# Forgetting attention and a SwiGLU block on one core: the seven-product output projection begins one token tile earlier, and three due times move

## The chip, the cores and the metric

The kernel runs on one core of a Trainium2 chip. The core has TensorE (PE, matrix products into PSUM), VectorE (DVE) and ScalarE (ACT), which read and write PSUM and SBUF, GpSimd (POOL), which here works on SBUF alone, and SyncE (SP), which issues DMAs. Each engine works through its own list of instructions in order. Semaphores make an instruction wait for another engine or for a DMA. The metric is the device time of one execution in microseconds, as the median of several runs.

## The reference

Inputs are q, k and v of 8 batches x 8 heads x 576 positions x 64, a forget gate f per position, and three weight matrices, w_gate and w_val (512 x 1536) and w_out (1536 x 512).

```python
scores = (1 / 8) * q @ k.T
cum    = cumsum(log(clip(f, 1e-4, 1)), axis=-1)
scores = where(causal, scores + cum[:, None] - cum[None, :], -1e9)
attn   = softmax(scores) @ v                          # per batch and head
x      = attn.transpose(0, 2, 1, 3).reshape(4608, 512)
g      = x @ w_gate
out    = (g * sigmoid(g) * (x @ w_val)) @ w_out       # 4608 x 512, float32
```

## The kernel before

The attention works on heads; a pair of heads shares one transposed tile of q and k (`QK`), with four more rows for the decay. Head h belongs to batch h // 8, pair p to batch p // 4. The scores of one head are computed with keys on the partitions, in four groups, called score banks here, each of which fills part of one PSUM bank (L703, `score`). ACT takes the exponent into `PT` or, for the first group, `PTa` (L737). POOL zeroes what lies above the diagonal (L746, `mask`). PE weighs the values with it (L760, `weigh`); a column of ones beside the values gives the denominator. DVE takes the reciprocal (L767) and scales (L772, into `xn`). The result is turned by a DMA transpose (L790, `cross`) or by PE (L777, `flip`, and a copy, `put`) into `xT`, the input of the second half. Two PSUM banks hold scores, one holds the weighed values, four serve the second half ("f"), one serves turning.

The loads of a pair p from 8 on have three steps: POOL issues DMAs that write q and k to DRAM as bf16 (L590, `narrow`); SP issues two DMA transposes from there into `QK` (L599, `turned`) and then a DMA for the decay rows (L602, `rows`).

The second half goes over nine tiles of 512 tokens, tiles 0 to 8. For each of 12 column blocks of 128 there are four matmuls with w_gate (`gp`) and four with w_val (`vp`), all L918; ACT takes the tanh (L922; Silu from tile 6 on, L925); DVE forms g * sigmoid(g) (L932, `silu`; not where ACT takes Silu) and multiplies (L935, `mul`) into `HH`. Two column blocks share one `HH` buffer.

The output projection of a tile comes in two forms. The plain form (`simple`, L976) has, for each of its two halves q and each of two token groups, 12 matmuls of 512 columns; ACT copies the result out of PSUM (L979), and SP stores it. The other form (`finish`, L969) computes a 2 x 2 block product with seven products in place of eight. For it, DVE adds parts of the activations (L960, `sums`: per `HH` buffer two of 512 columns and one of 256, into `SU`), and the weights are added once per run (L948 and L950, `blend`: six into `wt`, and four that overwrite quarters of `wo` and so come behind the last plain projection). Each product is six matmuls of 256 columns. ACT (L982), POOL (L989 `both`, L1014 `apart`) and DVE (L993 `more`, L1017 `close`) put the seven products together, and SP stores (L1020).

The order of all of this is made when the program is built, by the class `Plan`: a list of operations with engines, estimated durations, dependencies, buffers to take, a key and a time from which an operation may start (`ready`). It plays the list through and lets each engine take the ready operation with the lowest key; the order found is the order of the instructions in each engine's list. On the chip only the order is left: an operation starts when those before it on its engine are done and its semaphores allow it. Two of the times are of use below. `release(p)` is when the transposes of pair p become due, `release(p) - LEAD` when its narrowing DMAs do:

```python
release = lambda p: 0.0 if p < 2 * FB else PACE0 + min(p - 2 * FB, FB) * PACE_A + max(p - 3 * FB, 0) * PACE
for r in tails[:QUICK]:
    simple(*r)
blended = [op(..., blend, n, after=ready, key=BLEND_KEY + n, ready=BLEND_AT, ...) for n in range(6)]
blended += [op(..., blend, n, after=blended[:6] + plain, ...) for n in range(6, 10)]
for r in tails[QUICK:]:
    finish(*r, blended)
```

FB is 4, the pairs of a batch. With the constants before, pair 8 is due at 59.0, pair 12 at 95.0, and each later pair 8.6 after the one before it. Keys of activation sums (50000) and of weight sums (40000) are high, so DVE takes them when nothing else is ready.

Of the kernel before, what the change touches and what calls it, by code (L numbers as in the profile page):

```python
# [212 lines left out]
CROSS = (8, 9, 10)  # L213
PACE = 8.6
LATE = 2.5
PACE_A = 9.0
PACE0 = 59.0
LEAD = 14.0


@with_exitstack
def kernel(ctx, tc, q, k, v, f, w_gate, w_val, w_out, out):
# [81 lines left out]
    def op(eng, fn, *args, tag=None, packet=20.0, **kw):  # L304
        if not isinstance(eng, dict):
            eng = {eng[0]: eng[1]}
        o = plan.op(eng, lambda e: fn(e, *args), **kw)
        o.tag, o.packet = tag, packet
        return o
# [237 lines left out]
    for h, name, i in fixed + [(hqk[FB + p], "qk", 2 + p) for p in range(FB)]:  # L547
        h.pool, h.i = name, i
        plan.free[name].remove(i)
    release = lambda p: 0.0 if p < 2 * FB else PACE0 + min(p - 2 * FB, FB) * PACE_A + max(p - 3 * FB, 0) * PACE  # L550

# [127 lines left out]
    def queries(p, key):  # L679
        narrowed = [op(("POOL", SW), narrow, p, x, key=key - 200 + x, ready=release(p) - LEAD, dma=1.1, packet=900, tag=("narrow", p))  # L680
                    for x in range(2)]
        ts = []
        for x in range(2):
            ts.append(op(("SP", 1.45), turned, p, x, after=[narrowed[x], o_edge] + out1, behind=ts, take=[] if x else [hqk[p]],
                         use=[hqk[p]] if x else [], key=key, dma=1.6, ready=release(p), tag=("turned", p)))
        done = ts + [op(("SP", SPi), rows, p, after=ts + out0 + out1 + o_out2, use=[hqk[p]], key=key + 3, dma=0.25,
                        tag=("rows", p))]
        for j in range(2):
            q_ready[2 * p + j] = done
# [369 lines left out]
    def ffn(t, t0, n):  # L1059
        key, hs, ms = 1e5 * (t + 1), [None] * (KF // 2), []  # L1060
        for fc in range(KF):
            parts = [(0, HALF), (HALF, n - HALF)] if t == 0 and fc < WIDE else [(0, n)]
            ms.append([])
            for u, (lo, w) in enumerate(parts):
                lg, m = unit(t, fc, t0 + lo, w, hs, lo, key + 100 * fc + 50 * u, [last_gate[0]])
                ms[fc].append(m)
        last_gate[0] = lg
        tails.append((t, t0, key, hs, ms))
# [3 lines left out]
    def simple(t, t0, key, hs, ms):  # L1072
        for q in range(2):
            bo = Buf("ot")
            for h in range(2):
                bf, a = Buf("f"), None
                for g in range(0, KF // 2, 2):
                    a = op(("PE", mm(*[DM] * 4)), project, hs, q, h, bf, (g, g + 1),
                           after=[x for m in ms[2 * g : 2 * g + 4] for x in m] + [w_ready["o", c] for c in range(NCO)] + [a],
                           take=[] if g else [bf], use=[hs[g], hs[g + 1]] + ([bf] if g else []), key=key + 2000 + 200 * q + 100 * h + g, tag=("fo", t, q, h))  # L1080
                plain.append(a)
                c = op(("ACT", act(DM)), out_copy, h, bf, bo, after=[a] + (o_out2 + regrouped if t == 0 else []), take=[] if h else [bo],
                       use=[bf] + ([bo] if h else []), key=-4, tag=("ot", t, q, h))
                op(("SP", 0.7), store, t0 + h * HALF + q * P, h, bo, after=[c], use=[bo], key=-4, dma=1.0, packet=90, tag=("out", t, q, h))
# [92 lines left out]
    for t, t0 in enumerate(range(0, N_TOK, MT)):  # L1177
        ffn(t, t0, MT)
    for r in tails[:QUICK]:
        simple(*r)  # L1180
    ready = [w_ready["o", c] for c in range(NCO)]
    blended = [op({e: f((KF // 2) * HALF // 2) + 0.35 * (n // 2 == 1) for e, f in BLEND_ON.items()}, blend, n, after=ready, key=BLEND_KEY + n, ready=BLEND_AT, tag=("blend", n)) for n in range(6)]
    blended += [op({e: f((KF // 2) * HALF // 2) for e, f in BLEND_ON.items()}, blend, n, after=blended[:6] + plain, key=BLEND_KEY + n, ready=BLEND_AT, tag=("blend", n)) for n in range(6, 10)]
    for r in tails[QUICK:]:
        finish(*r, blended)
# [16 lines left out]

QUICK = 3


def F_POOLS(t):
# [19 lines left out]
BOTH_ON = {"POOL": pool2}  # L1228
APART_ON = {"POOL": pool2}
BLEND_ON = {"DVE": fast}  # L1230
BLEND_AT = 150.0
POOL_KEY = 50000
ALONE = (6, 6)
LAST_ON = {"DVE": slow}
# [126 lines left out]
```

## Time and profile before

| what | value |
|---|---|
| median of 3 runs (lowest to highest) | 378.81 us (378.62 to 379.19) |
| the profiled execution | 378.57 us |
| its span | 376.9 us |
| PE busy | 368.7 us, 98% |
| DVE busy | 248.9 us, 66% |
| ACT busy | 214.3 us, 57% |
| POOL busy | 161.4 us, 43% |
| granted TensorE clock | 1.00 in every stage |

The profile shows one execution. A row of a group gives line, engine, operation, tiles, shapes and count, then busy time in us and the mean duration of one in ns, then the idle time of the engine just before, and what ended it. A row of a time line gives start and duration in us. A shown matmul is longer than its share of TensorE's time, since the next one starts while it drains; from start to start is what counts. Busy shares are averages over stages with different limits. The stage up to about 288 us holds attention and tiles 0 to 6 side by side; what comes after is tiles 6 to 8 alone.

### The profile page before, as it was taken

Reading aid. Unit: us, or ns where it says so; the run is one execution under the profiler, and the core shown is the slowest. Engines: PE = TensorE matmul, PEld = TensorE weight load, DVE = VectorE, ACT = ScalarE, POOL = GpSimd, SP = SyncE. Lnnn points to the kernel's source line nnn. Section 1 sums busy time; section 2 is a strip of 40 time slices with the busy share of each in tenths; the row PEclk is TensorE's granted clock in tenths of the full one; section 3 lists DMA queues with packets and bytes.
Section 4 is the critical chain, followed back from the end, with each engine's and each line's share of the span. In section 5 each row is a group of like instructions: output and inputs, shape, how many; then the busy total and the mean of one; then the engine's idle time right before and its main releaser. Section 6 shows DMA issues by size and latency. Waiting matters only on the chain.

```text
span 376.9 us, 9094 instructions
## 1 busy us (share of the span) xinstructions
PE 368.7 (98%) x3427; PEld 233.7 (62%) x3427; DVE 248.9 (66%) x575; ACT 214.3 (57%) x438; POOL 161.4 (43%) x388
## 2 busy tenths in 40 slices
PE   8899999999999999999999999999999999999995
PEld 5667665455565555555685458655887776467464
DVE  7878986177526674499737994598638844753664
ACT  7999952265756754746576467555774433323322
POOL 8897547033633643465376437742462012003000
PEclk9999999999999999999999999999999999999999
DMA  8999998969988998998599999994225003002003
GB/s 147 192 197 195 207 200 151 167 117 176 177 186 169 199 164 151 227 189 183 117 155 206 220 132 165 241 222 95 60 73 93 2 2 111 2 0 89 25 0 114
DMA packets 125178, 52.01 MB, mean 138 GB/s; under 512 B 111838, under 2 KB 119710, under 8 KB 124366
## 3 DMA queue, kind: packets, MB, share of 16 engines
q1 hardware_dynamic: 108638, 36.08, 48.5%
q0 software_dynamic: 16288, 15.14, 27.2%
q8 instruction: 27, 0.44, 0.5%
q10 hardware_dynamic: 208, 0.20, 0.2%
q14 instruction: 17, 0.14, 0.1%
HBM read 38.56 MB, written 17.07 MB: 148 GB/s over the span
## 4 chain that ended last, share of the span: by engine, by line
PE 94%; DVE 2%; ACT 2%; issue 1%; POOL 0%; DVEq 0%
PE ps L918 49%; PE ps L969 14%; PE ps L703 10%; PE ps L976 8%; PE ps L760 8%; PE ps L721 1%; PE ps L777 1%; PE ps L578 1%; PE ps L729 0%; ACT QK L327 0%; ACT PT L737 0%; ACT PTa L737 0%; DVE hh L935 0%; ACT L530 0%; PE ps L1195 0%
## 5 line engine op out<-in xcount | busy, mean ns | idle before, releaser
L918 PE MATMUL ps<-xT,wv 128*128 128x512 bf16 (+2 forms) x496 | 111.8, 352 | 0.0
L918 PE MATMUL ps<-xT,wg 128*128 128x512 bf16 (+2 forms) x496 | 111.6, 352 | 0.0
L737 ACT ACTIVATE PT<-ps 128x384 bf16<-128x384 f32 (+2 forms) x192 | 91.7, 510 | 14.8 <-PE ps L703 9.7
L935 DVE SCALAR_TENSOR_TENSOR hh<-th,ps 128x512 bf16<-128x512 f32 (+1 forms) x112 | 74.5, 667 | 21.1 <-PE ps L918 12.9
L922 ACT ACTIVATE th<-ps 128x512 f32<-128x512 f32 (+1 forms) x82 | 47.2, 577 | 54.2 <-PE ps L918 51.8
L746 POOL TENSOR_SCALAR_AFFINE_SELECT PT<-PT 128x128 bf16<-128x128 bf16 (+1 forms) x192 | 54.1, 288 | 44.1 <-ACT PT L737 38.5
L918 PEld LDWEIGHTS <-wv 128*128 128x128 bf16 x496 | 45.0, 97 | 38.1
L918 PEld LDWEIGHTS <-wg 128*128 128x128 bf16 x496 | 45.1, 97 | 37.9
L932 DVE SCALAR_TENSOR_TENSOR th<-th,ps 128x512 f32<-128x512 f32 (+1 forms) x82 | 53.7, 656 | 19.7 <-ACT th L922 19.5
L703 PE MATMUL ps<-QK 68*128 68x256 bf16 x392 | 64.0, 261 | 0.4 <-ACT PTa L737 0.4
L746 POOL TENSOR_SCALAR_AFFINE_SELECT PTa<-PTa 128x256 bf16<-128x256 bf16 x64 | 26.3, 414 | 81.2 <-ACT PTa L737 80.4
L760 PE MATMUL ps<-VB,PT 128*128 128x65 bf16 x768 | 42.1, 193 | 0.0
L703 PEld LDWEIGHTS <-QK 68*128 68x128 bf16 x392 | 31.5, 97 | 14.0 <-issue 0.6
L760 PEld LDWEIGHTS <-PT 128*128 128x128 bf16 x768 | 34.2, 97 | 9.3 <-POOL PT L746 0.9
L737 ACT ACTIVATE PTa<-ps 128x384 bf16<-128x384 f32 x64 | 30.9, 487 | 15.6 <-PE ps L703 14.8
L767 DVE RECIPROCAL rc<-ps 128x5 f32<-128x5 f32 (+2 forms) x68 | 12.8, 188 | 40.4 <-PE ps L760 40.0
L969 PEld LDWEIGHTS <-su 128*128 128x128 bf16 x360 | 34.8, 97 | 4.6
L960 DVE TENSOR_TENSOR su<-hh 128x512 bf16<-128x512 bf16 (+1 forms) x108 | 36.7, 384 | 0.9
L925 ACT ACTIVATE th<-ps 128x512 f32<-128x512 f32 x30 | 17.9, 596 | 32.1 <-PE ps L918 32.1
L976 PE MATMUL ps<-wo,hh 128*128 128x512 bf16 x144 | 34.8, 379 | 0.0
L772 DVE TENSOR_TENSOR xn<-ps,rc 128x320 bf16<-128x320 f32 (+2 forms) x72 | 32.4, 454 | 2.2
L969 PE MATMUL ps<-wt,su 128*128 128x256 bf16 x216 | 28.8, 272 | 0.0
(97 smaller groups left out, 322.1 us busy)
## 6 DMA issues: line engine op xcount, KB each, us to landing
out_dram<-ot SPq DMA_DIRECT2D x34, 256.0 KB
natv<-in_v_dram SPq DMA_DIRECT2D x25, 256.0 KB
qk_d<-in_q_dram POOLq DMA_DIRECT2D x24, 144.0 KB, 3.6
qk_d<-in_k_dram POOLq DMA_DIRECT2D x24, 144.0 KB, 4.4
wv<-in_moe_w_val_dram POOLq DMA_DIRECT2D x3, 512.0 KB, 10.4
wg<-in_moe_w_gate_dram POOLq DMA_DIRECT2D x3, 512.0 KB, 12.2
wo<-in_moe_w_out_dram POOLq DMA_DIRECT2D x4, 384.0 KB, 13.8
VB<-in_v_dram POOLq DMA_DIRECT2D x7, 128.0 KB, 9.1
```

The lines of the kernel that those rows point to most:

```text
L703: nc.tensor.matmul(s[:, c : c + w], QK[:KR, hqk[p].i, 1, j * S + kt * P : j * S + (kt + 1) * P], QK[:KR, hqk[p].i, 0, j * S + q0 : j * S + ...
L737: nc.scalar.activation(place(h, i)[:, OFFS[i] : OFFS[i] + c], ps(bs)[:, :c], AF.Exp, scale=0.125)
L746: nc.gpsimd.affine_select(out=d, in_=d, pattern=pat, compare_op=ALU.is_ge, fill=0.0, base=0, channel_multiplier=-1,)
L760: nc.tensor.matmul(o[:, lo : lo + D + 1], pt[:, c : c + P], VB[hvb[b].i][:, kt, hb, : D + 1], start=first and n == 0, stop=last and n == l ...
L772: nc.vector.tensor_mul(XN[bx.i][:, qb : qb + nq, j], o, r)
L918: nc.tensor.matmul(ps(bf)[:, a:b], w[:, ko, fc * P : (fc + 1) * P], xT[:, ko, at : at + b - a], start=ko == 0 and a == 0, stop=ko == KD - ...
L922: nc.scalar.activation(TH[bt.i][:, :n], ps(bf)[:, :n], AF.Tanh, scale=0.5)
L932: nc.vector.scalar_tensor_tensor(out=t, in0=t, scalar=1.0, in1=ps(bf)[:, :n], op0=ALU.add, op1=ALU.mult)
L935: nc.vector.scalar_tensor_tensor(out=HH[bh.i][:, r, lo : lo + n], in0=TH[bt.i][:, :n], scalar=by, in1=ps(bf)[:, :n], op0=ALU.mult, op1=ALU ...
L960: E[e].tensor_tensor(out=o, in0=x, in1=y, op=f)
L969: nc.tensor.matmul(ps(bf)[:, c * HALF : (c + 1) * HALF], left(g)[:, q * P : (q + 1) * P], right[:, g], start=opens and g == 0, stop=g == K ...
L976: nc.tensor.matmul(ps(bf), HH[hs[g].i][:, r, lo : lo + P], wo[:, 2 * g + r], start=g + r == 0, stop=2 * g + r == KF - 1)
```

## The change

Six constants change; no function does. `QUICK`, the number of tiles with the plain projection, goes from 3 to 2, so tile 2 is projected with seven products. `BLEND_AT`, from which the weight sums may start, goes from 150 to 100. `PACE0` and `PACE_A` make pair 8 due at 57.0 instead of 59.0, with 8.8 instead of 9.0 from there to pair 12 (92.2 instead of 95.0), and 8.6 behind that as before. `LEAD` lets the narrowing DMAs be due 13.0 ahead of their pair instead of 14.0. Since the planner plays the whole list through anew, the order of instructions on all engines differs from where tile 1's projection and the third batch meet.

```diff
@@ -213,9 +213,9 @@
 CROSS = (8, 9, 10)
 PACE = 8.6
 LATE = 2.5
-PACE_A = 9.0
-PACE0 = 59.0
-LEAD = 14.0
+PACE_A = 8.8
+PACE0 = 57.0
+LEAD = 13.0
@@ -1202,7 +1202,7 @@
-QUICK = 3
+QUICK = 2
@@ -1228,7 +1228,7 @@
 BLEND_ON = {"DVE": fast}
-BLEND_AT = 150.0
+BLEND_AT = 100.0
 POOL_KEY = 50000
```

## The prediction

> **What bounds the kernel now.** I read the page first (busy shares, then the chain that ended last), then the table of stages, then the time lines of the few places where TensorE stood still.
>
> ```profile
> span 376.9 us, 9094 instructions
> PE 368.7 (98%) x3427; PEld 233.7 (62%) x3427; DVE 248.9 (66%) x575; ACT 214.3 (57%) x438; POOL 161.4 (43%) x388
> ...
> PE 94%; DVE 2%; ACT 2%; issue 1%; POOL 0%; DVEq 0%
> ```
>
> TensorE (PE) is the bound: 98% of the span, and 94% of the chain that ended last. The profiled execution took 378.57 us, 1.7 us more than its span; the median of the runs shown is 378.81, 0.24 above it. So the time after is this one's 378.57, less TensorE work removed, plus TensorE holes added, less holes that go; 0.24 on top gives the median. About 0.2% (0.76 us) is what a measurement of this kernel can tell from no change.
>
> The stages from 160 us on, columns window, width, busy time of PE, weight loads, DVE, ACT and POOL, then granted clock, DMA share, GB/s:
>
> ```profile
> 160.00:180.00 20.00, 19.44 (x147) 10.29 (x146) 19.06 (x39) 10.80 (x24) 11.52 (x25) 1.00 1.07 185
> 180.00:200.00 20.00, 19.48 (x219) 15.34 (x217) 10.66 (x28) 14.01 (x30) 12.30 (x30) 1.00 0.85 150
> 200.00:240.00 40.00, 39.88 (x366) 25.54 (x364) 29.06 (x63) 24.09 (x50) 21.95 (x54) 1.00 1.09 180
> 240.00:300.00 60.00, 60.00 (x609) 41.70 (x606) 45.30 (x100) 37.17 (x76) 22.86 (x59) 1.00 0.52 107
> ```
>
> VectorE (DVE) is full at 160 to 180 us, which is the stage of tile 3: ten weight sums, that tile's activation sums and the attention beside them. There and just behind it TensorE loses its time. On TensorE's time line the three places are these:
>
> ```profile
> 176.78 1.03 PE L918 MATMUL ps<-xT,wv 128*128 128x512 bf16 x4
> 178.37 0.25 PE L760 MATMUL ps<-VB,PTa 128*128 128x65 bf16 x3 [0.56 <-DVE xn L772]
> ...
> 182.27 0.55 PE L703 MATMUL ps<-QK 68*128 68x256 bf16 x4
> 183.18 0.33 PE L703 MATMUL ps<-QK 68*128 68x64 bf16 x2 [0.36 <-ACT PTa L737]
> 183.66 0.27 PE L760 MATMUL ps<-VB,PTa 128*128 128x65 bf16 x3 [0.15 <-POOL PTa L746]
> ...
> 208.89 1.03 PE L918 MATMUL ps<-xT,wv 128*128 128x512 bf16 x4
> 210.04 0.25 PE L760 MATMUL ps<-VB,PTa 128*128 128x65 bf16 x3
> ```
>
> Starts tell more than busy time here, since a matmul's shown end overlaps the next. Four matmuls of 512 columns take 4 x 0.216 = 0.86 us of TensorE (row of 20 below). From 176.78 to 178.37 are 1.59 us: 0.73 lost, waiting for the scaling of head 36 on DVE. From 208.89 to 210.04 are 1.15: 0.29 lost. At 182.27 two scores (0.38 us of work) are issued and the third, which needs the first one's PSUM bank, starts 0.91 after the first: 0.53 lost; its weighing comes another 0.31 late (183.66 less 183.18, less 0.17 of work). Together 1.86 us.
>
> **The change, part by part.** *Tile 2's projection.* A plain tile is 2 x 2 x 12 = 48 matmuls of 512 columns, a seven-product tile 2 x 7 x 6 = 84 of 256 (start us, duration, from the chain in order of time):
>
> ```profile
> 68.81 4.32 PE ps L976 x20
> ...
> 305.70 9.17 PE ps L969 x84
> ```
>
> 48 x 4.32/20 = 10.37 us become 9.17: **1.20 us less** on the path. This is the only certain gain. The 36 more weight loads lie under matmuls, as in the second row, where 84 run without a gap.
>
> *DVE work that comes with it.* Tile 2 gets 12 sums of 512, 6 of 256, two "more" and two "close":
>
> ```profile
> L960 DVE TENSOR_TENSOR su<-hh 128x512 bf16<-128x512 bf16 x72 | 28.4, 427 | 0.9
> ...
> L960 DVE TENSOR_TENSOR su<-hh 128x256 bf16<-128x256 bf16 x36 | 10.8, 299 | 0.0
> ...
> L1017 DVE TENSOR_TENSOR ot<-ps,ot 128x512 f32<-128x512 f32 x11 | 7.6, 690 | 16.0 <-POOL ot L1014 14.9 <-PE ps L703 0.9
> L993 DVE TENSOR_TENSOR ot<-ps,ot 128x256 f32<-128x256 f32 x12 | 5.1, 425 | 13.4 <-POOL ot L989 5.3 <-PE ps L969 4.1 <-POOL PTa L746 2.1
> ```
>
> 12 x 0.427 + 6 x 0.299 + 2 x 0.690 + 2 x 0.425 = 9.1 us. Against it the ten weight sums leave tile 3's stage:
>
> ```profile
> L948 DVE TENSOR_TENSOR wt<-wo 128x768 bf16<-128x768 bf16 x6 | 3.1, 550 | 0.0
> L948 DVE TENSOR_TENSOR wo<-wo 128x768 bf16<-128x768 bf16 x4 | 2.5, 662 | 0.0
> ```
>
> 5.6 us (and two small negations) move to tile 1's projection. The first six overwrite nothing and only wait for the weights; the last four overwrite parts of wo, so they stand behind tile 1's last plain matmul, and in the changed order one of them (0.66) is in front of the copy that tile 2's first gate projection needs. I take zero: hole A below, right there, covers it; without A it costs up to 0.66.
>
> *ACT, POOL, SP.* Four copies out of PSUM of 512 columns are replaced by four of the same form, nil. POOL gets two "both" and two "apart" (0.724 and 1.266 us each, 4.0 in all); POOL is at most 62% busy in these stages, so nil, at worst 1.27 when a mask stands behind an "apart". Tile 2's four stores wait on SP for "close" instead of an ACT copy, with pair loads and transposes queued behind them; tiles 3 to 5 do this now without a TensorE stall that a load caused, so nil, and the bad end is the second rival.
>
> *Due times.* Pairs 8 to 31 are due 2.0 to 2.8 us sooner. These are the planner's times: what they change is the order of instructions in each queue. I compared the two orders, counting each TensorE instruction at its columns (512 as 0.216 us). Narrowing DMAs pass some masks on POOL and transposes pass some stores on SP. The first scores of the third batch stand 3.5 us of TensorE work later, not sooner; those of pairs 16 and 18 stand 5.5 and 11.6 us sooner; the first gate projections move by -1.3 to +1.5 us.
>
> *Holes.* Old holes go with the old order: 1.86 us. For the new order I looked for a score too close behind the one whose bank it takes; 0.91 us is needed, from the row above, in which the exponent takes:
>
> ```profile
> 182.64 0.49 ACT L737 ACTIVATE PTa<-ps 128x384 bf16<-128x384 f32 x1 [0.43 <-PE ps L703]
> ```
>
> There are three such places. A: head 25, before tile 2's first gate projection, 0.45 us between, so 0.46 lost, and about 0.2 for the next score, since the exponents queue behind a copy of tile 1: 0.7. B: head 30, at tile 2's first product, 0.39 between: 0.52. C: head 49, at tile 4's first product, 0.54 between: 0.37. The ends are nil, if instructions between run late anyway, and 1.6 + 0.31 for each, as at 183.66; I take 1.59.
>
> Then DVE. Its time line in tile 3:
>
> ```profile
> 171.73 0.68 DVE L932 SCALAR_TENSOR_TENSOR th<-th,ps 128x512 f32<-128x512 f32 x1
> 172.52 0.69 DVE L935 SCALAR_TENSOR_TENSOR hh<-th,ps 128x512 bf16<-128x512 f32 x1
> ...
> 174.24 0.69 DVE L935 SCALAR_TENSOR_TENSOR hh<-th,ps 128x512 bf16<-128x512 f32 x1
> 174.85 1.25 DVE L960 TENSOR_TENSOR su<-hh 128x512 bf16<-128x512 bf16 x3
> 176.03 0.68 DVE L932 SCALAR_TENSOR_TENSOR th<-th,ps 128x512 f32<-128x512 f32 x1
> ...
> 177.61 0.18 DVE L767 RECIPROCAL rc<-ps 128x5 f32<-128x5 f32 x1
> 177.82 0.49 DVE L772 TENSOR_TENSOR xn<-ps,rc 128x320 bf16<-128x320 f32 x1
> ```
>
> From start to start: L932 to L935 0.79, L935 to the next 0.61, three sums 1.18. A column block of a seven-product tile (gate and value projection) costs DVE 0.79 + 0.61 + 1.18/2 = 1.99 us and TensorE 2 x 0.86 = 1.73. Where such blocks follow each other without attention between, DVE falls back. In the changed order tile 3 has six of them in a row; 6 x 0.26 is 1.6 us, some of it taken up by slack before. D: head 39's first weighing stands 0.82 us of work behind head 38's last, and the reciprocal and scaling between them need 0.21 + 0.21 + 0.49 even on an idle DVE; with a lag of 0.6 to 0.7 on DVE I take 0.75, near the 0.73 at 178.37 (ends 0.1 and 1.6). E: the same at the end of tile 2, head 30's first weighing: lag about 0.3, taken 0.26 (ends 0 and 0.8).
>
> **The sum.** 378.57 - 1.20 - 1.86 + 1.59 + 0.75 + 0.26 = 378.11; as a median 378.35, so 378.4.
>
> [...] The masks of 128 columns between 76 and 148 us, without activation sums, and between 168 and 282 us, with them:
>
> ```profile
> L746 POOL TENSOR_SCALAR_AFFINE_SELECT PT<-PT 128x128 bf16<-128x128 bf16 x32 | 9.4, 293 | 8.3 <-ACT PT L737 6.7
> ```
> ```profile
> L746 POOL TENSOR_SCALAR_AFFINE_SELECT PT<-PT 128x128 bf16<-128x128 bf16 x53 | 16.4, 310 | 11.8 <-ACT PT L737 10.2
> ```
>
> A mask is 17 ns longer beside sums, on average. [...]
>
> **The rivals.** *Faster:* D and E do not come, since without the weight sums DVE enters tile 3 unburdened. For it: the 160:180 row is full with 5.6 us of weight sums in it. Against it: the stretch of six blocks costs more DVE than TensorE whatever went before. 378.57 - 1.20 - 1.86 + 1.59 = 377.10, as a median 377.3.
>
> *Slower:* loads of pair 18 come late. Its SP rows and its score before, after those of pair 17:
>
> ```profile
> 150.80 0.64 SPq L602 DMA_DIRECT2D QK<-dec_d  x1
> ```
> ```profile
> 163.95 0.63 SPq L602 DMA_DIRECT2D QK<-dec_d  x1
> ```
> ```profile
> 171.48 0.55 PE L703 MATMUL ps<-QK 68*128 68x256 bf16 x4
> ```
>
> The decay rows are issued 12.8 us behind pair 17's due time (138.0), 17.4 behind pair 18's (146.6). Pair 18 becomes due at 143.8, and its score comes 11.6 us of work earlier, at 171.5 - 11.6 + 1.5 for A, B and E = 161.4. The closest load that stalled nothing was issued 4.6 us ahead of its score:
>
> ```profile
> 107.89 0.65 SPq L602 DMA_DIRECT2D QK<-dec_d  x1
> ```
> ```profile
> 112.47 0.33 PE L703 MATMUL ps<-QK 68*128 68x256 bf16 x2
> ```
>
> So rows issued later than 156.8, 13.0 behind the due time, stall TensorE: not at pair 17's distance (156.6), by 4.4 us at pair 18's (161.2). Against it: the new order issues them with less in front. The middle, 2.2, gives 380.6.
>
> [...]
>
> **How the numbers follow.** The forecast has 0.45 (own range 377.9 to 379.1; 0.07 of it faster by over 0.2%), the faster rival 0.32, late loads 0.13, masks 0.05; 0.05 is left, 0.02 faster and 0.03 slower. Faster 0.41, same 0.38, slower 0.21. The range takes in the faster rival with part of A to C gone (377.1) and reaches up to a load 1.6 us late (380.0).
>
> **What would show it.** Right: 84 products of tile 2 from about 142 us on, TensorE free of the waits at 178.37 and 183.18, and starts late by 0.4 to 0.7 us at heads 25, 30, 39 and 49; DVE below 19 us in the stage of tile 3. Wrong: a wait of TensorE on DVE longer than 1 us in tile 2 or 3; a first score waiting for QK; or no holes at all, with the full 3 us gained.

## The result, and the profile after

The changed kernel takes **379.69 us** (median of 12 runs, 379.06 to 380.46) against 378.79 (378.26 to 379.43, 12 runs) for the kernel before: a ratio of 1.0023, 95% interval 1.0014 to 1.0032. It is slower by 0.90 us, where 378.4 was forecast. Its profiled execution took 379.06 us, the shortest of its twelve, with a span of 377.0. The page after:

```profile
span 377.0 us, 9186 instructions
PE 368.4 (98%) x3463; PEld 237.2 (63%) x3463; DVE 257.6 (68%) x597; ACT 214.3 (57%) x438; POOL 164.7 (44%) x392
...
PE 87%; DVE 7%; DMA 2%; issue 1%; ACT 1%; POOL 1%; DVEq 0%; ACTq 0%; POOLq 0%
```

TensorE is still the bound, but VectorE's share of the chain that ended last has gone from 2% to 7%. (The 2% of DMA is a load of k in the first 11 us.) The table of stages of the changed kernel, same columns as in the prediction:

```profile
100.00:120.00 20.00, 19.64 (x183) 11.51 (x182) 11.23 (x27) 13.53 (x29) 10.98 (x29) 1.00 0.91 175
120.00:140.00 20.00, 20.00 (x144) 10.48 (x143) 18.63 (x38) 11.10 (x23) 8.84 (x23) 1.00 0.98 172
140.00:160.00 20.00, 19.33 (x237) 15.65 (x236) 9.89 (x26) 13.59 (x30) 12.87 (x32) 1.00 0.87 161
160.00:180.00 20.00, 19.87 (x135) 10.13 (x133) 18.12 (x38) 9.26 (x19) 8.82 (x20) 1.00 1.14 200
180.00:200.00 20.00, 19.06 (x214) 15.09 (x212) 9.70 (x23) 14.05 (x30) 13.12 (x34) 1.00 0.83 160
```

and two rows of the kernel before that were not shown yet:

```profile
100.00:120.00 20.00, 20.00 (x190) 11.66 (x189) 6.37 (x16) 12.03 (x26) 9.67 (x29) 1.00 0.82 170
...
140.00:160.00 20.00, 20.00 (x172) 11.40 (x171) 9.32 (x22) 12.01 (x26) 7.51 (x22) 1.00 0.90 183
```

At 160 to 180 us TensorE has won 0.43 us of busy time. At 100 to 120, 140 to 160 and 180 to 200 it has lost 0.36, 0.67 and 0.42. The places on TensorE's time line of the changed kernel, with A, B, D and E named as in the prediction:

```profile
114.14 0.30 PE L703 MATMUL ps<-QK 68*128 68x320 bf16 x1
114.79 0.71 PE L703 MATMUL ps<-QK 68*128 68x256 bf16 x4 [0.35 <-ACT PT L737]
...
141.73 0.55 PE L703 MATMUL ps<-QK 68*128 68x256 bf16 x4
142.64 0.33 PE L703 MATMUL ps<-QK 68*128 68x64 bf16 x2 [0.36 <-ACT PTa L737]
142.81 0.82 PE L969 MATMUL ps<-wo,hh 128*128 128x256 bf16 x6
143.89 0.25 PE L760 MATMUL ps<-VB,PTa 128*128 128x65 bf16 x3 [0.27 <-DVE xn L772]
...
165.88 1.03 PE L918 MATMUL ps<-xT,wg 128*128 128x512 bf16 x4
167.04 0.25 PE L760 MATMUL ps<-VB,PTa 128*128 128x65 bf16 x3
...
184.01 0.82 PE L969 MATMUL ps<-wo,hh 128*128 128x256 bf16 x6
185.77 0.25 PE L760 MATMUL ps<-VB,PTa 128*128 128x65 bf16 x3 [0.94 <-DVE xn L772]
```

Starts less TensorE's work, as before. A: the score at 114.79 comes 0.65 after one of 0.14: 0.51 lost, and 0.16 more at the next. B: 0.91 less 0.38, which is 0.52 before rounding. C: 0.20 and 0.13 late at 225.53 and 225.91, ahead of tile 4's first product. E: six products of 256 columns are 0.65 us (84 in 9.17, the prediction's row); head 30's weighing comes 1.08 after them: 0.43 lost, and 0.21 at a score behind it. D: 1.76 less 0.65 is **1.11 us**, the largest loss from 40 us on. At 167.04 stands one that the prediction did not list: head 37's weighing, 0.29 late.

Adding up every matmul's start less its work from 40 us on, TensorE loses 3.89 us in the profile before and 5.50 after. The work of a matmul of c columns is counted here as the planner has it, c / 2400 + 0.0025 us, which gives the 0.216 us for 512 columns and the 0.109 for 256 of the prediction's rows. VectorE's time line of the changed kernel shows what D waits for:

```profile
179.65 0.68 DVE L932 SCALAR_TENSOR_TENSOR th<-th,ps 128x512 f32<-128x512 f32 x1
...
183.62 0.67 DVE L932 SCALAR_TENSOR_TENSOR th<-th,ps 128x512 f32<-128x512 f32 x1
184.40 0.69 DVE L935 SCALAR_TENSOR_TENSOR hh<-th,ps 128x512 bf16<-128x512 f32 x1
185.00 0.19 DVE L767 RECIPROCAL rc<-ps 128x5 f32<-128x5 f32 x1
185.22 0.49 DVE L772 TENSOR_TENSOR xn<-ps,rc 128x320 bf16<-128x320 f32 x1
```

VectorE has no gap. Head 38's last weighing is issued ahead of 184.01, but its reciprocal stands behind the `silu` and the `mul` of tile 3's last column block and starts at 185.00, some 0.95 us after it could. Followed back from 186 us to 166, some 70% of the chain are VectorE's:

```profile
by line: DVE hh L935 24.7%; DVE th L932 21.3%; PE ps L918 17.3%; DVE su L960 16.4%; issue 7.9%; DVE xn L772 5.0%; PE ps L760 4.3%; DVE rc L767 2.0%; DVEq L935 0.7%; PE ps L703 0.7%
```

### The profile page after: what moved, and what is told of

Same layout as the page of the kernel before. It is cut to its first block, busy times and chain, and to the rows that moved or that the text cites. A ratio compares the mean times of both kernels' runs of the same rounds, so it can differ in the third digit from the quotient of the medians.

```text
span 377.0 us, 9186 instructions
## 1 busy us (share of the span) xinstructions
PE 368.4 (98%) x3463; PEld 237.2 (63%) x3463; DVE 257.6 (68%) x597; ACT 214.3 (57%) x438; POOL 164.7 (44%) x392
## 4 chain that ended last, share of the span: by engine, by line
PE 87%; DVE 7%; DMA 2%; issue 1%; ACT 1%; POOL 1%; DVEq 0%; ACTq 0%; POOLq 0%
PE ps L918 44%; PE ps L969 16%; PE ps L703 10%; PE ps L760 8%; PE ps L976 5%; DVE hh L935 2%; DVE th L932 2%; DMA su<-in_k_dram 2%; DVE su L960 1%; PE ps L721 1%; PE ps L578 1%; ACT PT L737 1%; PE ps L777 1%; DVE xn L772 1%; POOL su L554 1%
## 5 line engine op out<-in xcount | busy, mean ns | idle before, releaser
L746 POOL TENSOR_SCALAR_AFFINE_SELECT PT<-PT 128x128 bf16<-128x128 bf16 (+1 forms) x192 | 53.3, 284 | 45.1 <-ACT PT L737 39.2
L932 DVE SCALAR_TENSOR_TENSOR th<-th,ps 128x512 f32<-128x512 f32 (+1 forms) x82 | 53.6, 654 | 17.4 <-ACT th L922 16.9
L960 DVE TENSOR_TENSOR su<-hh 128x512 bf16<-128x512 bf16 (+1 forms) x126 | 43.7, 391 | 1.2
L969 PEld LDWEIGHTS <-su 128*128 128x128 bf16 x420 | 40.0, 98 | 5.2
L760 PE MATMUL ps<-VB,PT 128*128 128x65 bf16 x768 | 41.2, 193 | 0.0
L969 PE MATMUL ps<-wt,su 128*128 128x256 bf16 x252 | 33.5, 272 | 0.0
L989 POOL TENSOR_TENSOR ot<-ot 128x256 f32<-128x256 f32 x12 | 8.7, 724 | 48.2 <-ACT ot L982 48.1
```

The source lines that it names most:

```text
L746: nc.gpsimd.affine_select(out=d, in_=d, pattern=pat, compare_op=ALU.is_ge, fill=0.0, base=0, channel_multiplier=-1,)
L760: nc.tensor.matmul(o[:, lo : lo + D + 1], pt[:, c : c + P], VB[hvb[b].i][:, kt, hb, : D + 1], start=first and n == 0, stop=last and n == l ...
L932: nc.vector.scalar_tensor_tensor(out=t, in0=t, scalar=1.0, in1=ps(bf)[:, :n], op0=ALU.add, op1=ALU.mult)
L960: E[e].tensor_tensor(out=o, in0=x, in1=y, op=f)
L969: nc.tensor.matmul(ps(bf)[:, c * HALF : (c + 1) * HALF], left(g)[:, q * P : (q + 1) * P], right[:, g], start=opens and g == 0, stop=g == K ...
```

## The experiments

Theory 1: the loss is VectorE's lag in the column blocks of tiles 2 and 3, which comes out as late weighings. Theory 2: it is the new order as such, scores too close and loads too late. Theory 3, added after the first runs: the new due times alone make it (some expectations use this number for another rival, which they name). Theory 4, last: a part of it lies outside the span. Each group of runs had its own runs of the kernel before; medians of these were 378.63, 378.86, 378.83 and 378.58.

**The changed kernel again.** No edit.

> The changed kernel unaltered, once more: the profile on record is of the shortest of its twelve executions. From 40 us on its trace holds 0.45 us more than that of before (holes of 5.5 against 3.85 us, matmul work 1.2 less). Theory 1 (these holes are the loss): 0.4 to 0.6 us slower than before in this call, 379.1 to 379.3, with the same late starts at heads 25, 30, 37, 39 and 48. Theory 3 (something from execution to execution, such as late loads, adds to it): 0.9 slower again, and a late start in the new profile that is not in the old.

379.95 us (379.31 to 380.39), ratio 1.0021 [1.0011, 1.0031]: above theory 1's 379.1 to 379.3, and 1.09 above the kernel before, as the rival had it. Its profile has the same late starts and another, between the gate and value projections of tile 3:

```profile
178.96 1.03 PE L918 MATMUL ps<-xT,wv 128*128 128x512 bf16 x4
180.15 1.02 PE L918 MATMUL ps<-xT,wg 128*128 128x512 bf16 x4 [0.16 <-DVE th L932]
```

1.19 less 0.86 is 0.33, and 0.17 at 176. Here VectorE's lag has grown until TensorE's next block waits 0.16 us for L932, the step that reads a gate projection out of its PSUM bank. Of five profiles of this order, two are without it and three have 0.33 to 0.50; from 40 us on they lose 5.50, 6.01, 5.87, 5.87 and 5.51 us, 5.75 on average.

What differs between these executions is one pair of sums on VectorE, beside a cast of v to bf16 on GpSimd (L329). This run first, then the profile on record:

```profile
170.01 1.26 DVE L960 TENSOR_TENSOR su<-hh 128x512 bf16<-128x512 bf16 x2
170.03 0.62 POOL L329 CAST VB<-natv 128x512 bf16<-128x512 f32 x1
```
```profile
169.21 0.76 DVE L960 TENSOR_TENSOR su<-hh 128x512 bf16<-128x512 bf16 x2
169.54 0.89 POOL L329 CAST VB<-natv 128x512 bf16<-128x512 f32 x1 [0.32 <-DMA natv<-in_v_dram]
```

The pair took 0.76 us in both profiles without the loss, and 1.17, 1.17 and 1.26 in the three with it. That is five of five, but no run changes it alone.

**VectorE's work taken away, the order kept.** In `sums`, with `NARROW` the tiles 2 to 8, or 2 and 3, or 3 to 8 on the kernel before. Each sum is formed in 32 of its 256-column parts alone and the rest is left out; `SU` is cleared ahead, among the weight sums:

```diff
...
+        if t in NARROW:
...
+                           (u[:, 2:4, :32], h[:, :, HALF : HALF + 32], h[:, :, :32], ALU.subtract),
+                           (u[:, 4, :32], h[:, 0, :32], h[:, 1, HALF : HALF + 32], ALU.add))[n]
+            E[e].tensor_tensor(out=o, in0=x, in1=y, op=f)
+            return
```

> The changed kernel with its instruction order kept, but each activation sum on VectorE formed in 32 of its 256-column parts alone (from tile 2 on; six clears of the sum buffers are put in front of the first six weight sums). The sums' values are left out in the other columns. Theory 1, VectorE falls behind beside the sums: the late starts at the weighings of heads 30, 37 and 39 (0.64, 0.29 and 1.10 us in the changed kernel's trace) go, those of heads 25, 30 (its third score) and 48, which come from the order, stay: about 2.0 us less than the changed kernel, 377.7. Theory 2, the loss lies in the order and in late loads: at most 0.3 us less, 379.4.

> As the first, but only the sums of tiles 2 and 3 are thin (their values are left out in the other columns), so VectorE is relieved where the two largest late starts are. Theory 1: heads 30, 37 and 39 as in the first, so 377.7 to 377.9. Theory 2: 379.4. If it comes out between, tiles 4 and 5 have a share that the profiled run does not show.

All tiles thin: 378.42, ratio 0.9998 [0.9984, 1.0012]; tiles 2 and 3 alone: 378.59, 1.0001 [0.9987, 1.0015]. Either wins back the whole loss, and what the later tiles do adds nothing that can be told. It is less than theory 1's 377.7 to 377.9: with tiles 2 and 3 thin the late starts add up to 4.77 us against 5.75. A, B and C stay to 0.01 us. E's 0.43 is gone, head 37's 0.29 is 0.11. D falls from 1.11 to 0.44, as TensorE's and VectorE's time lines of the first one show (its L977 is L969):

```profile
185.69 0.82 PE L977 MATMUL ps<-wo,hh 128*128 128x256 bf16 x6
186.79 0.25 PE L760 MATMUL ps<-VB,PTa 128*128 128x65 bf16 x3 [0.27 <-DVE xn L772]
```
```profile
185.41 0.69 DVE L935 SCALAR_TENSOR_TENSOR hh<-th,ps 128x512 bf16<-128x512 f32 x1 [0.21 <-PE ps L918]
186.02 0.19 DVE L767 RECIPROCAL rc<-ps 128x5 f32<-128x5 f32 x1
```

VectorE now has gaps and is not late. The 0.44 that stay are order: the reciprocal stands in VectorE's list behind the `mul` of the last block, and that waits for TensorE. So lag is the cause of 0.67 of D's 1.11. The score behind E, 0.21, stays too, and the late starts at head 24 and at 275 us: order as well. The thin pair ahead of D takes 0.29 us, where the wide one of the changed kernel takes 0.91 beside masks and the three wide pairs before it 0.76 each; so these runs do not tell VectorE's own work from the 0.15 us that this pair takes longer beside masks.

The same on the kernel before, with the clears among the weight sums, and again with the clears beside copies near 65 us:

> The kernel before with its order kept and the same thin sums (tiles 3 on), so the sums' values are left out in most columns. Theory 1: the waits for scaling at 178 and 210 us (0.73 and 0.29) go, the late scores at 183 us stay: 377.8. Theory 2: within 0.3 us of the kernel before, 378.6. By theory 1 the two thin kernels stand against each other as TensorE work and order alone would have it: the changed one lower by 0.1 to 0.6 us; by theory 2 the changed one stays higher by 0.9.

> The kernel before with thin sums: the sums of the halves of tiles 3 to 8 are formed in 32 of their 256 columns (the rest of each pool is zero, cleared beside the copies of pairs 6 and 7, ahead of token tile 3), so the values computed from them are left out. Every matmul stays. In the kernel before, 0.73 us at 178.4 (head 37 waits for the scaling of head 36) and 0.29 us at 210 are late starts of the matmuls behind VectorE. If VectorE's lag is what they are made of (theory 1), they go and the time falls to 377.6 to 377.9. If the time is a matter of the order and of the loads (theory 2), it stays at 378.6 +- 0.3.

378.48, ratio 0.9995 [0.9984, 1.0006], and 378.72, 1.0002 [0.9990, 1.0014]. Theory 1 had 377.6 to 377.9. The times decide nothing, since the clears made new late starts: 1.06 us at 153 and 164 in the first; 1.13 at 66 in the second, behind three clears on VectorE of 1.94 us. But where the old 0.73 and 0.29 stood TensorE no longer waits:

```profile
177.92 1.03 PE L921 MATMUL ps<-xT,wv 128*128 128x512 bf16 x4
178.79 0.25 PE L760 MATMUL ps<-VB,PTa 128*128 128x65 bf16 x3
```

0.87 us from start to start, which is the work.

**The reciprocal and the scaling ahead of `silu` and `mul`.**

```diff
-            br, a = norm(h, bo, ws, nq, key - 1)
+            br, a = norm(h, bo, ws, nq, -6 + 1e-4 * h)
...
-                             take=[] if scaled else [bx], use=[br, bo] + ([bx] if scaled else []), key=key - 1, tag=("scale", h)))
+                             take=[] if scaled else [bx], use=[br, bo] + ([bx] if scaled else []), key=-6 + 1e-4 * h, tag=("scale", h)))
```

> The changed kernel with one edit: the reciprocal and scaling of a head from 8 on come ahead of gate and value products on VectorE whenever both are ready, where they came behind. Theory 1: the late starts at heads 30, 37 and 39 that waited for a scaling (0.43, 0.29, 1.10) shrink by the multiplications that stood in front, about 1.2 us in all, and part of it comes back as products and sums that are late: 378.6 to 379.2. Theory 2: the order of scores and loads decides, unchanged at 379.5 to 379.9.

379.90, ratio 1.0025 [1.0013, 1.0038]: nothing gained, as theory 2 had it. E's 0.43 is gone (head 30's weighing is now 0.32 late, behind a mask), but at D the scaling still got its place behind the same `mul`, presumably because VectorE is free earlier in the plan than on the chip:

```profile
187.19 0.25 PE L760 MATMUL ps<-VB,PTa 128*128 128x65 bf16 x3 [0.94 <-DVE xn L772]
```

0.42 and 0.33 stand between projections at 176 and 180, and 0.64 at 211. The lag isn't removed by serving one of its victims first; it comes out at the next.

**The change in halves.** Tile 2's projection and the sooner weight sums with the old due times; then the due times alone:

```diff
-QUICK = 3
+QUICK = 2
...
-BLEND_AT = 150.0
+BLEND_AT = 100.0
```
```diff
-PACE_A = 9.0
-PACE0 = 59.0
-LEAD = 14.0
+PACE_A = 8.8
+PACE0 = 57.0
+LEAD = 13.0
```

> Seven products from tile 2 on and the weight sums from 100 us, with the due times of the kernel before. TensorE work is that of the changed kernel. Theory 1: VectorE is as loaded in tiles 2 and 3 as with the change, so there are late starts there again; the order is another. From the order alone, tile 2's first product stands 1.4 us behind the last instruction that TensorE can do before it, and tile 4's 1.3, so it is the slowest of all, 380.5 to 381.5. If the due times made the loss, it is faster than the changed kernel, below 379.

> The changed due times (PACE_A 8.8, PACE0 57, LEAD 13) with three plain tiles and the old place of the weight sums (QUICK = 3, BLEND_AT = 150). The written order then has tile 2 with 48 wide matmuls again (+1.2 us), head 25 late by some 0.6 us and tile 3's first product by some 0.45, while 0.84 + 0.3 us of late starts of the kernel before are gone from it. Theory 1 (what was lost lies in VectorE's lag in tile 3's six dense column blocks, whatever the due times): 378.7 to 379.0. Theory 3 (the new due times themselves make the loss): 379.7 or more, the same as the changed kernel.

380.14, ratio 1.0035 [1.0022, 1.0048], and 380.66, ratio 1.0055 [1.0040, 1.0070]. The second half alone is slower than both together; the first is by its median, but the intervals overlap. The first lies below theory 1's 380.5 to 381.5, since the holes at the first products of tiles 2 and 4 came as 0.63 each and not as 1.4 and 1.3. The second is as theory 3 has it and against theory 1's number: D stands in it at full size, without tile 2's products and with the weight sums at their old place, and a like one at tile 4:

```profile
184.37 0.82 PE L969 MATMUL ps<-wo,hh 128*128 128x256 bf16 x6
186.13 0.25 PE L760 MATMUL ps<-VB,PTa 128*128 128x65 bf16 x3 [0.94 <-DVE xn L772]
```
```profile
216.87 0.30 PE L703 MATMUL ps<-QK 68*128 68x320 bf16 x1
218.26 0.25 PE L760 MATMUL ps<-VB,PTa 128*128 128x65 bf16 x3 [1.09 <-DVE xn L772]
```

So it is the due times that bring six column blocks in a row (169 to 180 us in this run and in the changed kernel) and the weighings where the lag hits them. With the old due times tile 3 has three blocks in a row, as in the kernel before, and the weighing behind its first product is on time, 0.66 us behind it. There VectorE is late in tile 2: a weighing at 138.65 starts 0.85 late and waits for a scaling, and three sums from 130.42 on, beside casts and masks on GpSimd, take 2.05 us, where three without GpSimd take 0.96 (at 164.01 in the changed kernel).

**VectorE's costs in the planner.** The trace shows 0.79 us from `silu` to the `mul` that reads it, where independent steps of that size follow after 0.61; and 427 and 299 ns for the sums. The planner counted less. With these costs alone, and with due times chosen anew for them, for two and for three plain tiles:

```diff
-                        push(busy[e], "done", (o, e, True))
+                        push(busy[e] + (0.17 if isinstance(o.tag, tuple) and o.tag[0] == "silu" else 0.0), "done", (o, e, True))
...
-    return (n / 2 + 110) / 960
+    return (n / 2 + 163) / 960
```
```diff
-PACE = 8.6
+PACE = 8.61
...
-PACE_A = 8.8
-PACE0 = 57.0
+PACE_A = 8.63
+PACE0 = 58.4
...
-BLEND_AT = 100.0
+BLEND_AT = 90.0
```

The second diff is that for two plain tiles; for three, PACE0 is 55.2, PACE_A 9.37, PACE 8.45, LEAD 12.5, and BLEND_AT stays at 100.

> The changed kernel with its own due times (PACE_A 8.8, PACE0 57, LEAD 13, BLEND_AT 100, QUICK 2), and only VectorE's costs in the planner made those of the profile. The written order puts some 2.5 us of late starts into the plan. Theory 1 (the planner's too short costs of VectorE's steps are what the changed kernel lost by): 378.0 to 378.5. Theory 3 (the due times chosen again are what f3 gained by, the costs alone give nothing): 379.5 to 380.

> Seven products from tile 2 on, with the planner told what VectorE takes here: 0.17 us more between gate and value product of a block, 0.055 more for a sum. Due times chosen anew for it (58.4, 8.63, 8.61, weight sums from 90). Theory 1: the late starts that the order does not show go, those that it shows stay, about 2.3 us after 100 us: 378.6 - 1.2 - 2.0 + 2.3 = 377.7. Theory 2: as the changed kernel, 379.5.

> The same kernel as f3: two plain tiles, VectorE's costs in the planner as the profile shows them (0.17 us from silu to the product that reads it, two-input bf16 sums longer by 0.055 us), and due times chosen again (PACE0 58.4, PACE_A 8.63, BLEND_AT 90). Theory 1: 377.2 to 377.6 once more, and a profile without the late start at 250 that f3's had, with 2.0 to 2.8 us of late starts from 40 us on. Theory 3 (f3's time was a matter of the chip or of lucky runs): 378.5 or more.

> Seven products from tile 3 on, as before, with the same true costs and due times chosen anew (55.2, 9.37, 8.45, weight sums from 100). The order shows 1.15 us of late starts after 100 us. Theory 1: 378.6 - 2.0 + 1.15 = 377.8, equal to the kernel with two plain tiles although TensorE has 1.2 us more of matmuls: then VectorE, not TensorE, sets the pace where attention and seven products lie side by side. Theory 2: at or above the kernel before.

The costs alone: 378.53, ratio 0.9995 [0.9985, 1.0004]. That is 1.2 us less than the changed kernel by two constants of the plan (0.2 of it outside the span, see below), and its interval lies clear of the changed kernel's; theory 1 had 378.0 to 378.5. E's 0.43, the late starts in the dense stretch and head 37's are gone, and D is down to 0.44 (1.09 less 0.65):

```profile
184.34 0.82 PE L969 MATMUL ps<-wo,hh 128*128 128x256 bf16 x6
185.43 0.25 PE L760 MATMUL ps<-VB,PTa 128*128 128x65 bf16 x3 [0.27 <-DVE xn L772]
```

How VectorE keeps up shows in its list: a sum now stands between a `silu` and the `mul` that reads it.

```profile
172.25 0.69 DVE L932 SCALAR_TENSOR_TENSOR th<-th,ps 128x512 f32<-128x512 f32 x1
172.85 0.28 DVE L960 TENSOR_TENSOR su<-hh 128x256 bf16<-128x256 bf16 x1
173.05 0.68 DVE L935 SCALAR_TENSOR_TENSOR hh<-th,ps 128x512 bf16<-128x512 f32 x1
...
175.70 0.69 DVE L932 SCALAR_TENSOR_TENSOR th<-th,ps 128x512 f32<-128x512 f32 x1
```

The six blocks in a row are still there, but two of them with three sums take 3.45 us of VectorE, no more than TensorE's 16 x 0.216 = 3.46, against 3.77 to 3.97 in the changed kernel. There 67 of 82 `silu` have their `mul` right behind them and none a sum; here 33 have the `mul` and 29 a sum.

With the due times too, two plain tiles: 377.36, ratio 0.9952 [0.9936, 0.9968], and again 377.10, **0.9958 [0.9945, 0.9971]: it beats both kernels.** The late starts are 3.24 us, more than the 2.0 to 2.8 expected. D is nil here: the weighing comes 0.66 after six products.

```profile
182.85 0.82 PE L969 MATMUL ps<-wo,hh 128*128 128x256 bf16 x6
183.51 0.26 PE L760 MATMUL ps<-VB,PTa 128*128 128x65 bf16 x3
```

Three plain tiles: 378.43, ratio 0.9993 [0.9979, 1.0007], and not theory 1's 377.8, equal to two. So tile 2's seven products are worth having, 1.1 us between the two medians of one group of runs (377.36 and 378.43; the due times differ too), once the order does not spend it.

**What is outside the span.** The time less the span is 1.66 to 1.85 us in the runs of the kernel before that were made beside these versions, and 2.00 to 2.10 in all twelve of the changed one. Small instructions were added to one engine's list in a late tile, the order left as it is:

```diff
...
+            for n in range(16 if len(pads) == 10 else 0):
+                nc.gpsimd.memset(spare, 0.0)
```
```diff
...
+        for n in range(8 if len(pads) == 20 else 0):
+            nc.scalar.activation(warm, warm, AF.Copy)
```
```diff
...
+        for n in range(16 if len(pads) == 10 else 0):
+            nc.vector.memset(spare, 0.0)
```

The fourth has the first one's edit, with 13 clears, on the kernel before.

> The changed kernel with 16 more small clears on GpSimd in tile 6, where it has time; the order of everything else is the same. Theory 4 (the time outside the span follows the place where an engine's list of instructions ends): it moves by 0.1 us or more from the changed kernel's 2.0 to 2.1. Against it: it stays at 2.0 to 2.1, and the time at 379.7 +- 0.3.

> The changed kernel with 8 more one-element copies on ScalarE in a late tile. Theory 4: the time outside the span moves by 0.1 us or more from 2.0 to 2.1, towards the 1.7 to 1.85 of the other versions (their ScalarE lists are 1 to 15 instructions longer). Against it: it stays, and the time at 379.7 to 380.2.

> The changed kernel with 16 more one-element clears on VectorE in tile 6. Theory 4: the time outside the span moves by 0.1 us or more from 2.0 to 2.1. Against it: it stays, and the time rises by no more than 0.5, since VectorE has time there.

> The kernel before with 13 more small clears on GpSimd late in the run, which gives GpSimd as many instructions as in the changed kernel. Theory 4, with GpSimd's list as the cause: the time outside the span rises from 1.66 to 1.85 to 2.0 or more, and the time from 378.8 to 379.1. Against it: both stay.

GpSimd: 1.99 to 2.10, no move. VectorE: 1.99 to 2.08, no move. The kernel before with GpSimd's list as long as the changed one's: 1.68 to 1.79, no move. **ScalarE: 1.75 to 1.86**, 0.25 less than without the eight copies. So of these lists only ScalarE's moved it. It isn't a matter of more or fewer: by the records in the trace the list has 710 instructions before (1.73 us), 695 after (2.05), 691 in the first half of the change (1.72), 696 with the true costs (1.84), 699 with the scaling first (1.95), 703 here (1.80). What happens there stays open. The totals, 380.40 (ratio 1.0045), 379.48 (1.0022), 379.53 (1.0027) and 378.84 (0.9999), differ by more than this part does, presumably by what the first 40 us and the dense stretch do in each execution; the first lies above its expected 379.7 +- 0.3.

**All of it in one sum.** TensorE's work is 1.19 us less where tile 2 has seven products. The span before has a median of 377.0 us. Then 377.0 less that work, plus the late starts from 40 us on above 3.9, should give every version's span. Some traces lack 33 to 38 matmul records; 0.216 us for each, as for 512 columns, is taken off their late starts:

| version | late starts of one profile, us | span by the sum | median span | time less span | median time |
|---|---|---|---|---|---|
| changed (mean of five profiles) | 5.75 | 377.7 | 377.6 | 2.05 | 379.69 |
| old due times | 6.18 | 378.1 | 378.4 | 1.72 | 380.14 |
| due times alone | 5.86 | 379.0 | 378.9 | 1.75 | 380.66 |
| sums thin in tiles 2 and 3 | 4.77 | 376.7 | 376.6 | 2.03 | 378.59 |
| true costs alone | 4.64 | 376.6 | 376.7 | 1.84 | 378.53 |
| true costs, new due times, again | 3.24 | 375.2 | 375.3 | 1.82 | 377.10 |
| the same, three plain tiles | 3.41 | 376.5 | 376.6 | 1.74 | 378.43 |

It holds within 0.3 us, though it sets one profile beside a median, so nothing large is missing.

## Why the prediction was wrong

The time lay inside the given range, but on the other side of the kernel before. By its steps, late starts from the profile on record:

| step | predicted | measured |
|---|---|---|
| tile 2's projection | -1.20 | -1.19 |
| old holes go | -1.86 | -1.86, none of the four is at its place |
| A, B, C | 0.70, 0.52, 0.37 | 0.67, 0.52, 0.33 |
| D: lag | 0.66 | 0.67 |
| D: without any lag | 0.09 | 0.44 |
| E: lag | 0.26 | 0.43 |
| E: the score behind it | 0 | 0.21 |
| not listed: head 37's weighing | 0 | 0.29, of it lag 0.18 |
| not listed: the dense stretch of tile 3 | 0 | lag, 0 to 0.50, here 0 (mean of five profiles 0.23) |
| not listed: head 24, a score at 275 us | 0 | 0.18, 0.27 |
| all other late starts (the rest of 5.50 less 3.89) | 0 | -0.53 |
| around the span, "1.7 us" | 0 | 0.32 (2.05 for 1.73, medians) |

The rows add up to -0.46 predicted and 0.75 measured, or 1.0 with the mean of five profiles; the medians differ by 0.90. D's two parts are the prediction's 0.75 taken apart: 0.82 us between where 0.91 is needed, and a lag of 0.6 to 0.7.

**The step that failed is the one on VectorE, D and E, in two ways.** First, it counted the lag only where a first weighing waits for a scaling. The price of a column block, 1.99, came here only where masks of GpSimd lie beside the sums: from 179.65 to 183.62 are 3.97 us for two blocks, but from 175.88 to 179.65 only 3.77, 1.89 each. The row of three sums that it was taken from (1.25) lay beside masks; without GpSimd three take 0.96. The lag at D came out as said all the same, which is in part luck: the prediction took 0.6 to 0.7 out of 6 x 0.26 us without a sum. But the lag was 0.43 and not 0.26 at E, and it came out at two kinds of place that were not searched: a weighing that had more room (head 37) and the blocks themselves, where TensorE waits for L932 (0.16 us at 180.15 in the changed kernel's second profile). Together 1.5 us of lag in place of 0.92; thin sums, which take the lag away and leave the order, won back 1.0 in late starts and 1.1 in time. Second, "0.21 + 0.21 + 0.49 even on an idle DVE" is not what an unhurried VectorE gives at D: in its list the reciprocal stands behind the last block's `mul`, which TensorE has to feed first. That is 0.44 for 0.09. The prediction looks at VectorE's list for the blocks, not for what stands right ahead of each reciprocal. Of both, 0.9 us was too little, and the -1.20 and most of the -1.86 were eaten.

The other error is the 1.7 us around the span, taken over as a constant. It costs 0.3 of the 0.9, and no row of the trace before shows that it would change.

The faster rival had the sign wrong: six blocks in a row do cost more VectorE than TensorE in this order, without the weight sums ahead, and the argument noted against it decided. "Whatever went before" is too strong, since with sums between `silu` and `mul` they don't. Late loads did not come: no wait of TensorE on a load into `QK` is among those of the changed kernel, and its longest behind the start is D's.

```profile
PE ps L760 <- DVE xn L772: 1.2, 2, 0.9
PE ps L1195 <- DVE warm L523: 1.1, 1, 1.1
```

To masks that come late beside tile 2's sums the prediction gave 0.05; no run shows a mask of tile 2 made late by a sum, and among the waits of TensorE in the changed kernel none is for a mask. Of the tile's 18 sums 14 lie between 120 and 142 us, and the masks of 128 columns there take 292 ns on average, where the prediction's row without sums has 293:

```profile
L746 POOL TENSOR_SCALAR_AFFINE_SELECT PT<-PT 128x128 bf16<-128x128 bf16 x7 | 2.0, 292 | 1.0 <-ACT PT L737 0.6
```

Single masks do take longer, which the means of 293 and 310 ns hide. Beside the weight sums at 100 to 120 us two masks of 128 columns take 597 and 604 ns, and eleven 347 on average:

```profile
L746 POOL TENSOR_SCALAR_AFFINE_SELECT PT<-PT 128x128 bf16<-128x128 bf16 x11 | 3.8, 347 | 0.5
```

In tiles 2 and 3 it is VectorE's sums that take longer: tile 2's take 453 and 360 ns on average (512 and 256 columns) against 427 and 299 in the prediction's row, and the pair at 181.16, ahead of D and beside masks, 0.91 us against 0.76 for the three pairs before it. The masks of 128 columns in tile 3, from 162 to 186 us, take 299 ns on average. So it is the sums more than the masks that take longer there: part of VectorE's lag is this, how much of it no run shows. A mask that TensorE waits for came in both profiles of the fastest version: 0.43 late at 115.85 in the second, behind a mask of 599 ns beside a weight sum.

Of the signs named ahead, the 84 products from 142.81 on, VectorE under 19 us in tile 3's stage (18.12), the old waits gone, and late starts at heads 25, 30, 39 and 49 came, though 39's 1.11 and 49's 0.33 lie outside the 0.4 to 0.7. One of those for wrong came as well, a loss of over 1 us to VectorE in tile 3: 1.11 by the starts, of which the profile calls 0.94 a wait.

## What to carry to other kernels

When an engine beside the bound one needs more time per block than the bound one (here 1.89 to 1.99 against 1.73 us), the lag adds up through every such block in a row; look for it at every later place where the bound engine needs something from that engine, its free buffers included, and for each such place read what stands right ahead of the needed step in that engine's list. Serving the late step first only moves the loss; less work on that engine, or a plan that knows its real costs, removes most of it, here by putting an independent step between two that depend on each other. Take an instruction's cost where no other engine works beside it (three sums took 0.96 us there, 1.25 beside masks), and look at single instructions, since a mean hides the few that take twice as long (eleven masks of 347 ns on average had two of 597 and 604 among them). Where an order is planned from costs, compare these with starts in the trace, dependent pairs above all, before choosing due times: two constants were worth 1.2 us here and due times chosen on top of them 1.4 more, while each half of the change alone lost 1.5 to 1.8 against the kernel before.

## What was not expected of the hardware

- Time outside the span differs by version, 1.72 to 2.05 us, is steady within 0.1 to 0.2 for most of them, and fell by 0.25 us with eight more instructions in ScalarE's list, while longer lists of GpSimd and VectorE did not move it.
- The same kernel can differ by 3.7 us between two profiled executions: 380.22 and 376.52 for the true costs with new due times. In the slower one a transfer of q was late at the start, and TensorE's granted clock was 0.50 from 10 to 12 us and 0.69 from 12 to 14, where the faster one had 1.00 from 8 to 16; from the slower one's time line and its table of stages:

```profile
9.02 0.66 PE L562 MATMUL ps<-ident,su 64*64 64x64 bf16 x36 [1.53 <-DMA su<-in_q_dram]
```
```profile
10.00:12.00 2.00, 2.00 (x22) 1.29 (x21) 0.82 (x2) 1.98 (x4) 0.84 (x2) 0.50 2.30 158
12.00:14.00 2.00, 2.00 (x67) 1.61 (x64) 0.57 (x1) 1.42 (x4) 1.41 (x3) 0.69 1.64 199
```

  The longest single gap there is 1.53 us; what lowered the clock no run shows. That start cost 1.8 us of TensorE's time against the other execution, and a late transfer of decay rows at 250 us another 1.5:

```profile
252.19 0.56 PE L703 MATMUL ps<-QK 68*128 68x256 bf16 x4 [1.36 <-DMA QK<-dec_d]
```

  It did not come in the second profile of that kernel, so it is a matter of the execution and not of the order alone.
- A VectorE step on 512 columns from PSUM whose result the next one reads costs 0.79 us from start to start, against 0.61 where the next reads something else: 0.18 us per dependent pair, 67 such pairs in the changed kernel.
- Where VectorE's sums and GpSimd's casts and masks lie side by side, some of either take longer: a pair of sums 0.91 and 1.26 us, with 0.76 usual, a cast 0.89 us, with 0.62 usual, and two masks beside weight sums 597 and 604 ns, with 292 usual. The longest is a sum of 256 columns in the run with the old due times, 1.36 us beside two casts at 138.51, where 0.28 is usual.
